# Fewer, longer loads in a two-round decode kernel: 85 transfers where there were 101, and other records kept on the chip

## The chip, the core and the metric

The kernel runs on one core of one Trainium2 chip. The metric is the device time of one execution in microseconds, less is better. The time before is the median of three runs, 712.61 us (712.23 to 714.89). One further execution was recorded by the hardware profiler; all views of the profile in this document are of that execution, or of one like it.

## The reference

One token for each of four batch entries goes twice through the same pair of layers: attention over the last 1,024 positions of a cache, with 32 heads of 128, and a two-matrix MLP with a ReLU. All is float32. What is computed, cut to what matters:

```python
def _A_ref(x, k_cache, v_cache, wq, wo):          # x: 4 x 1 x 640, wq: 640 x 4096, wo: 4096 x 640
    q = (x @ wq).reshape(4, 1, 32, 128).transpose(0, 2, 1, 3)
    k = k_cache[:, :, Sk - W:, :]                 # 4 x 32 x 1024 x 128
    v = v_cache[:, :, Sk - W:, :]
    p = softmax(einsum("bhqd,bhkd->bhqk", q, k) * 128 ** -0.5)
    return einsum("bhqk,bhkd->bhqd", p, v).transpose(0, 2, 1, 3).reshape(4, 1, 4096) @ wo

def _B_ref(x, w1, w2):                            # w1: 640 x 1728, w2: 1728 x 640
    return maximum(x @ w1, 0) @ w2

x = x + _A_ref(layernorm(x), k_cache, v_cache, wq, wo)
x = x + _B_ref(layernorm(x), w1, w2)
x = x + _A_ref(layernorm(x), k_cache, v_cache, wq, wo)
x = x + _B_ref(layernorm(x), w1, w2)
```

## The kernel before

**Records.** The host packs everything that one head needs into a record of `REC` = 9,472 float32 columns on 128 partitions: 640 columns of the query weights, 4,096 of keys (from `K`), 4,096 of values (from `V` = 4,736) and 640 of the output weights (from `WO` = 8,832, "wo" below). One record is 4.85 MB. The two MLP matrices are another 17,280 columns, `wm`. The weights and the cache are needed twice, and the core's memory holds about five and a half records, so nearly all of it is read twice: 32 records and the MLP in round 0, then again in round 1. What is still on the chip when round 1 begins is not read again: round 1 takes the heads in the order 27 to 31, then 0 to 26 (`order`, line 177), so that the last five records of round 0 serve first.

**Places.** `store` (line 139) has five places of one record, `NS`; `home(h, r)` (line 180) gives the place of a record. `ring` (line 142) has 4,832 columns for the MLP's weights of round 0 and for parts of the first new records of round 1. `kept` and `kept2` (lines 140 and 141) hold the last 2,176 columns of records 26 and 5 from round 0 to round 1, entered in `at` (line 186) so that round 1 finds them there.

**Transfers.** All loads are issued on SP's queue, in one fixed order, `items`. The planner code of lines 231 to 283 fills the list before anything is computed: whole records, `group`s that cut several records into longer transfers (`FIVE` cuts five records into three; rows of up to 15,872 columns), the `ending` of a round in smaller pieces, the MLP's pieces (`MLP_RING`, `W1_SLOT`, `W2_SLOT`), and at the start of round 1 a stream that is cut to the places as the five old records leave them (`IN_RING`, `IN_SLOT`, `places`). `pump` (line 285) issues the head of the list as long as its columns are free; `done` and `free` release columns in the program's order as TensorE has read them. SP issues strictly in order: a transfer whose place is not yet free holds all behind it. A consumer waits for the whole transfer that brings its columns.

**Compute.** For each head TensorE makes the query (`query`, PE into `misc`), the scores (`scores`, into one of two `sc_ps`), then after the softmax (`softmax`, `weights`: DVE and ACT) the values (`values`, into `o_ps`), a transposition (`output_T`) and the projection with wo into `acc` (`project`). The loop of line 517 is skewed: in the turn of record n it issues scores of n+1, values of n, query of n+2, `output_T` and `project` of n. In round 0 the wo of the last `LATE` = 6 heads come after everything else of the round, and their projections follow at the end (lines 553 to 560). In the turn of the last but two record four small matmuls of `busy` (line 354) follow the values. `park` (line 326) copies the tail of the last K part out of the spare place into PSUM, so that MLP weights can be loaded there. Then `center` and `mlp` follow; in round 0 the five blocks of w1 free their places one by one, and the next pieces of the MLP are loaded into them.

The same InOrder helper records each instruction, so most rows of the profile have the line L105; groups are told apart by tile names.

Of the kernel before, what the change touches and what calls it, by code (L numbers as in the profile page):

```python
# [32 lines left out]
F32 = mybir.dt.float32  # L33
# [5 lines left out]
P = 128  # L39
B, D, H, DH, W, FF = 4, 640, 32, 128, 1024, 1728  # L40
NB = 4
FD = D // NB
# [5 lines left out]
REC = 2 * D + 8 * W  # L48
# [12 lines left out]
SIXTH = 5  # L61
KEPT2 = WO - 3 * 512
# [24 lines left out]
LAST_FIVE = [REC + 4736, 2 * REC - 4736, REC, REC]  # L87
GROUPS = [{6: FOUR, 10: FIVE, 15: FIVE, 20: FIVE}, {9: FIVE, 14: FIVE, 19: LAST_FIVE}]
# [24 lines left out]
def decode_kernel(ctx: ExitStack, tc: tile.TileContext, xf, rec, wm, out):  # L113
# [65 lines left out]

    def home(h, r):  # L180

        return h % NS if not r or h >= LAST else (h - 6 + LAST) % NS
# [6 lines left out]
    buffers = {"store": store, "ring": ring, "kept": kept, "kept2": kept2}  # L189
# [4 lines left out]
    def place(buf, col):  # L194
        return ("store", spare * REC + FROM + col) if buf == "spare" else (buf, col)
# [11 lines left out]
    def piece(r, h, lo, hi, buf="store", col=None):  # L207
        run(r, h * REC + lo, h * REC + hi, buf, home(h, r) * REC + lo if col is None else col)


    def group(r, h, sizes):
        lo = 0
        for size in sizes:
            run(r, h * REC + lo, h * REC + lo + size, "store", home(h, r) * REC + lo)
            lo += size

    def ending(r, hs, late):
        a, b, c = hs[-3:]
        end = WO if late else REC
        last = WO if late else KEPT  # L220
        for h, lo, hi in ((a, 0, V), (b, 0, V), (a, V, end), (c, 0, V), (b, V, end), (c, V, V + VH), (c, V + VH, last)):
            piece(r, h, lo, hi)
        if late:
            for h in hs[-1:] + hs[-LATE:-1]:
                if h == LAST - 1:
                    piece(r, h, WO, REC, "kept", WO - KEPT)
                else:
                    piece(r, h, WO, REC)
# [3 lines left out]
    piece(0, hs[0], 0, V)  # L232
    piece(0, hs[0], V, REC)
    group(0, 1, FOUR)
    for h in hs[5:-3]:
        if h in GROUPS[0]:
            group(0, h, GROUPS[0][h])
        if any(g <= h < g + sum(z) // REC for g, z in GROUPS[0].items()):
            continue
        piece(0, h, 0, KEPT if h == LAST - 1 else KEPT2 if h == SIXTH else WO if h >= H - LATE else REC)  # L240
        if h == SIXTH:
            piece(0, h, KEPT2, REC, "kept2", 0)
        if h == LAST - 1:
            piece(0, h, KEPT, WO, "kept", 0)
# [10 lines left out]
    for lo, hi, buf, col in IN_RING:  # L255
        piece(1, new[0], lo, hi, *place(buf, col))
    places = [("store", old[i] * REC + lo, old[i] * REC + hi) for i, lo, hi in (
        (0, 0, K), (0, K + 1024, K + VH), (0, K + VH + 1024, V), (1, 0, K + VH), (1, K + VH, V), (0, V, WO), (0, WO, REC),
        (2, 0, V), (1, V, REC), (3, 0, V), (2, V, REC), (4, 0, FROM), (3, V, REC),
        (4, FROM + PARKED, REC), (4, FROM, FROM + PARKED))] + [("ring", 0, RING)]  # L260
    stream = [(new[0], lo, hi) for lo, hi in IN_SLOT] + [(h, 0, KEPT2 if h == SIXTH else REC) for h in new[1:6]]
    for buf, lo, hi in places:
        while stream:
            h, c, end = stream[0]
            cut = max(x for x in [*CUTS, end] if x <= min(end, c + hi - lo))
            if cut <= c:
                break
            piece(1, h, c, cut, buf, lo)
            lo += cut - c
            stream[:1] = [(h, cut, end)] if cut < end else []  # L270
    assert not stream
# [6 lines left out]
    for ks in W1_SLOT:  # L278
        weight(1, ks[0] * FF, (ks[-1] + 1) * FF, "store", home(LAST + 1, 0) * REC + ks[0] * FF)
    n = 0  # L280
    for size in W2_SLOT:
        weight(1, W2 + n * FD, W2 + (n + size) * FD, "store", home(LAST + 2, 0) * REC + n * FD)
        n += size
# [42 lines left out]
    def park(i):  # L326
        a = spare * REC + FROM
        to, lo, hi = ((misc, 0, 512), (sc_ps[1], 512, 1536), (o_ps, 1536, 2048))[i]
        act.copy(to, store[:, a + lo:a + hi])
        free("store", a + lo, a + hi)  # L330
        pump()

    def unpark(i):
        b = home(LAST, 0) * REC
# [6 lines left out]
        if i == 3:  # L341
            c = spare * REC
# [259 lines left out]
```

## Time and profile before

| | before |
|---|---|
| runs, us | 712.23, 712.61, 714.89 |
| profiled execution, us | 711.53 |
| its span, first to last instruction, us | 709.7 |
| PE, DVE, ACT busy, us | 503.7, 317.4, 101.4 |
| read from HBM, MB | 301.61 |
| packets on SP's queue | 14,544 |

The profiled execution took 711.53 us, of which the span is 709.7 us; 1.8 us lie around the span. It is 1.1 us under the median of the runs. Engines in the profile: PE is TensorE's matmul, DVE VectorE, ACT ScalarE, SPq the queue that issues loads. A row of the timeline has the start, the duration, the engine, line, operation, tiles, shape and count, and in brackets the idle time before it and what ended that.

### The profile page before, as it was taken

The page shows a single profiled execution, that of the slowest core. Times are in us where ns is not written, and L with a number is a line of the kernel's source. Part 1 is how long each engine was busy: PE and PEld are TensorE (multiplying, and loading weights), DVE is VectorE, ACT ScalarE, POOL GpSimd, SP SyncE. Part 2 cuts the span into 40 slices and gives each one's busy share as a digit, 9 for nine tenths or more (in the row PEclk, how much of TensorE's full clock was granted, in tenths as well). Part 3 has the DMA queues.
Part 4 walks back from the last instruction along what each step waited for, and adds up shares of the span by engine and source line. Part 5 has one row for each costly group of instructions (what it writes and reads, how often), then busy time and mean ns, then how long its engine had stood idle before and what let it go on. Part 6 is the DMA issues. An engine that isn't in the chain of part 4 may idle for free.

```text
span 709.7 us, 8716 instructions
## 1 busy us (share of the span) xinstructions
PE 503.7 (71%) x3722; PEld 203.4 (29%) x3722; DVE 317.4 (45%) x647; ACT 101.4 (14%) x216; POOL 1.1 (0%) x9
## 2 busy tenths in 40 slices
PE   4388386478566578879878898675577686776885
PEld 2123132232232223333313333231222231233322
DVE  3244253253443453545641866634244252453661
ACT  0111010011010110111120321201011011011120
POOL 0000000000000000000000000000000000000000
PEclk9987787577787776877999999968677676897899
DMA  9999999999999999999999999999999999999997
GB/s 400 421 453 408 454 410 459 417 439 441 428 433 426 424 451 420 424 425 430 427 408 408 417 435 422 448 425 453 428 428 437 439 432 430 432 427 419 427 425 303
DMA packets 14614, 302.24 MB, mean 426 GB/s; under 512 B 1632, under 2 KB 2032, under 8 KB 6256
## 3 DMA queue, kind: packets, MB, share of 16 engines
q1 hardware_dynamic: 14544, 301.69, 99.2%
q8 instruction: 29, 0.48, 0.2%
q14 instruction: 9, 0.07, 0.0%
q10 hardware_dynamic: 32, 0.01, 0.0%
HBM read 301.61 MB, written 0.08 MB: 425 GB/s over the span
## 4 chain that ended last, share of the span: by engine, by line
DMA 73%; PE 21%; DVE 3%; issue 1%; ACT 1%; another core or an unknown queue 0%; SPq 0%; ACTq 0%; DVEq 0%
DMA store<-rec 67%; PE o_ps L105 8%; PE sc_ps L105 7%; DMA store<-wm 3%; DMA ring<-wm 3%; PE misc L105 3%; PE acc L105 3%; DVE scratch L105 1%; DVE o_ps L105 1%; ACT oTs L105 1%; DVE small L105 0%; DVE store L105 0%; PE t_ps L105 0%; SPq L105 0%
## 5 line engine op out<-in xcount | busy, mean ns | idle before, releaser
L105 PE MATMUL sc_ps<-store,qT 128*4 128x512 f32 x1014 | 190.6, 837 | 24.4 <-DMA store<-rec 22.4
L105 PE MATMUL misc<-xT,store 128*128 128x4 f32 x620 | 97.2, 283 | 121.4 <-DMA store<-rec 121.1
L105 PE MATMUL o_ps<-store,scratch 128*16 128x512 f32 x954 | 143.8, 680 | 2.2 <-DMA store<-rec 1.2
L105 PEld LDWEIGHTS misc<-xT,store 128*128 128x128 f32 x620 | 91.8, 230 | 178.5 <-DMA store<-rec 145.7
L105 DVE TENSOR_REDUCE small<-sc_ps 128x1 f32<-128x1024 f32 x64 | 78.3, 1224 | 139.9 <-PE sc_ps L105 139.9
L105 ACT ACTIVATE sc_ps<-sc_ps,small 128x1024 f32<-128x1024 f32 (+1 forms) x68 | 71.1, 1046 | 319.6 <-DVE small L105 318.3
L105 DVE STREAM_TRANSPOSE sc_ps<-sc_ps 128x1024 f32<-128x1024 f32 (+1 forms) x70 | 81.7, 1167 | 0.1
L105 DVE TENSOR_TENSOR qT<-misc,rows 128x4 f32<-128x4 f32 x61 | 9.5, 155 | 135.6 <-PE misc L105 135.6
L105 DVE TENSOR_TENSOR o_ps<-o_ps,of_block 128x512 f32<-128x512 f32 x62 | 43.3, 699 | 52.3 <-PE o_ps L105 50.9
L105 PEld LDWEIGHTS o_ps<-store,scratch 128*16 128x16 f32 x954 | 33.3, 114 | 114.4 <-issue 101.1
L105 PEld LDWEIGHTS sc_ps<-store,qT 128*4 128x4 f32 x1014 | 32.5, 106 | 107.8 <-issue 65.4
L105 PE MATMUL acc<-store,oTs 128*4 128x160 f32 x478 | 34.3, 368 | 17.2 <-ACT oTs L105 16.4
L105 DVE TENSOR_REDUCE scratch<-o_ps 128x128 f32<-128x512 f32 x62 | 42.9, 691 | 2.1
L105 ACT COPY oTs<-o_ps 128x4 f32<-128x4 f32 x62 | 10.1, 162 | 226.6 <-PE o_ps L105 226.6
L105 PE MATMUL o_ps<-rows,scratch 128*128 128x4 f32 x124 | 27.0, 288 | 13.2 <-DVE scratch L105 13.0
L105 PEld LDWEIGHTS o_ps<-rows,scratch 128*128 128x128 f32 x124 | 22.8, 229 | 20.8 <-DVE scratch L105 17.7
L105 DVE TENSOR_TENSOR scratch<-sc_ps,mrt 128x128 f32<-128x128 f32 (+1 forms) x70 | 19.6, 280 | 2.7
L105 DVE TENSOR_SCALAR mrt<-of_batch,small 128x4 f32<-128x4 f32 x64 | 14.7, 229 | 2.2
L105 PE MATMUL acc<-kept,small 128*1 128x344 f32 (+1 forms) x44 | 14.7, 445 | 0.0
L105 PEld LDWEIGHTS acc<-store,oTs 128*4 128x4 f32 x478 | 6.6, 84 | 23.2 <-ACT oTs L105 21.2
L105 DVE STREAM_TRANSPOSE scratch<-small 128x32 f32<-128x32 f32 x64 | 12.8, 201 | 0.8 <-ACT sc_ps L105 0.8
L105 ACT ACTIVATION_READ_ACCUMULATOR sc_ps<-sc_ps,small 128x1 f32 x64 | 12.3, 193 | 0.0
(86 smaller groups left out, 118.1 us busy)
## 6 DMA issues: line engine op xcount, KB each, us to landing
store<-rec SPq DMA_DIRECT2D x10, 7872.0 KB, 28.9
store<-rec SPq DMA_DIRECT2D x5, 7936.0 KB, 33.4
store<-rec SPq DMA_DIRECT2D x14, 2368.0 KB, 27.3
store<-rec SPq DMA_DIRECT2D x6, 4736.0 KB, 26.7
store<-rec SPq DMA_DIRECT2D x4, 6336.0 KB, 27.7
store<-rec SPq DMA_DIRECT2D x2, 7104.0 KB, 29.7
store<-rec SPq DMA_DIRECT2D x2, 6272.0 KB, 43.6
store<-rec SPq DMA_DIRECT2D x2, 4416.0 KB
```

Source lines behind the costliest of these rows:

```text
L105: r = build(*args, **kwargs)
```

## The change

The number of transfers goes from 101 to 85, with the same bytes. Part by part:

- One tile `store` takes the place of `store`, `kept` and `kept2`: `FIRST` = 2,176 columns ahead, five places, 2,176 columns behind. Records 0 to 4 of round 0 lie at column 0 and on, so that the first 2,176 columns of record 0 stay where they were loaded and round 1 finds them there. Records 20 to 24 lie 2,176 columns higher than the others, so that the last 2,176 columns of record 24 end behind the fifth place and stay. Records 26 and 5 are no longer kept. `busy` reads `store`'s first columns in place of `kept`'s.
- Round 0: all records from 0 to 24 come in five groups of `FIVE`, 25 to 27 (27 without wo) in two transfers (`THREE_LATE`), 28 in one, 29 in one, which `ending` before had cut into keys and values with the keys of 30 between them. `LATE` is 5: the wo of record 26 comes with its record and is projected in its turn.
- Round 1: record 0 in four pieces of the ring, two kept parts and its wo; records 1 to 5 as one stream cut to the freed places, across records; 6 to 8 in two transfers (`THREE`) in place of three. Record 24 in one transfer where there were two, record 26 in full. `W1_SLOT` joins blocks 2 and 3.

```diff
-KEPT2 = WO - 3 * 512
+FIRST = K + 3 * 512
...
-IN_RING = [(640, 1152, "ring", 4256), (1152, 3200, "spare", 0), (3200, 4736, "ring", 0), (4736, 6272, "ring", 1536),
-           (6272, 7296, "ring", 3072), (8832, 8992, "ring", 4096)]
-IN_SLOT = [(0, K), (7296, WO), (8992, REC)]
+IN_RING = [(2176, 2688, "ring", 4256), (2688, 4736, "spare", 0), (4736, 6272, "ring", 0), (6272, 8832, "ring", 1536)]
...
-W1_SLOT = [[0, 1], [2], [3], [4]]
+W1_SLOT = [[0, 1], [2, 3], [4]]
...
-LATE = 6
+LATE = 5
...
-FOUR = [REC + 3200, REC + 3072, 2 * REC - 6272]
 FIVE = [REC + 6272, 2 * REC - 3072, 2 * REC - 3200]
 LAST_FIVE = [REC + 4736, 2 * REC - 4736, REC, REC]
-GROUPS = [{6: FOUR, 10: FIVE, 15: FIVE, 20: FIVE}, {9: FIVE, 14: FIVE, 19: LAST_FIVE}]
+THREE = [REC + HALF, REC + HALF]
+THREE_LATE = [REC + 4224, REC - 4224 + WO]
+GROUPS = [{h: FIVE for h in range(0, 25, 5)} | {25: THREE_LATE}, {6: THREE, 9: FIVE, 14: FIVE, 19: LAST_FIVE}]
...
-    store = sb.tile([P, NS * REC], F32, name="store")
-    kept = sb.tile([P, REC - KEPT], F32, name="kept")
-    kept2 = sb.tile([P, REC - KEPT2], F32, name="kept2")
+    store = sb.tile([P, FIRST + NS * REC + REC - KEPT], F32, name="store")
...
     def home(h, r):
-        return h % NS if not r or h >= LAST else (h - 6 + LAST) % NS
+        if r:
+            return FIRST + (h if h >= LAST else h - 6 + LAST) % NS * REC
+        return (0 if h < NS else FIRST + REC - KEPT if h // NS == 4 else FIRST) + h % NS * REC
...
-    at = {("rec", 1, LAST - 1): [(KEPT, REC, "kept", 0)], ("rec", 1, SIXTH): [(KEPT2, REC, "kept2", 0)]}
+    at = {("rec", 1, LAST - 3): [(KEPT, REC, "store", FIRST + NS * REC)], ("rec", 1, 0): [(0, FIRST, "store", 0)]}
...
     def ending(r, hs, late):
         a, b, c = hs[-3:]
         end = WO if late else REC
-        last = WO if late else KEPT
-        for h, lo, hi in ((a, 0, V), (b, 0, V), (a, V, end), (c, 0, V), (b, V, end), (c, V, V + VH), (c, V + VH, last)):
+        for h, lo, hi in ((a, 0, WO if late else KEPT), (b, 0, V), (c, 0, V), (b, V, end), (c, V, V + VH),
+                          (c, V + VH, end)):
             piece(r, h, lo, hi)
...
     hs = order[0]
-    piece(0, hs[0], 0, V)
-    piece(0, hs[0], V, REC)
-    group(0, 1, FOUR)
-    for h in hs[5:-3]:
+    for h in hs[:-3]:
         if h in GROUPS[0]:
             group(0, h, GROUPS[0][h])
...
+    piece(0, hs[-4], 0, WO)
     ending(0, hs, True)
...
-    stream = [(new[0], lo, hi) for lo, hi in IN_SLOT] + [(h, 0, KEPT2 if h == SIXTH else REC) for h in new[1:6]]
+    cuts = [h * REC + x for h in new[1:6] for x in CUTS]
+    c, end = new[1] * REC, new[6] * REC
     for buf, lo, hi in places:
...
+        if lo == old[0] + WO:
+            piece(1, new[0], WO, REC, buf, lo)
+        elif c < end:
+            cut = max(x for x in cuts if x <= min(end, c + hi - lo))
+            run(1, c, cut, buf, lo)
+            c = cut
...
-            pe.matmul(to[32 * g:32 * g + 1, :n], ones, kept[:, :n], start=to is not spare_cols, stop=True,
+            pe.matmul(to[32 * g:32 * g + 1, :n], ones, store[:, :n], start=to is not spare_cols, stop=True,
```

More of the change, by code (lines that the diff above doesn't have):

```diff
@@ L194, in place @@
     def place(buf, col):
-        return ("store", spare * REC + FROM + col) if buf == "spare" else (buf, col)
+        return ("store", spare + FROM + col) if buf == "spare" else (buf, col)
     def weight(r, lo, hi, buf, col):
@@ L224, in ending @@
             for h in hs[-1:] + hs[-LATE:-1]:
[L225 to L228, printed above, removed]
+                piece(r, h, WO, REC)
     hs = order[0]
-    piece(0, hs[0], 0, V)
-    piece(0, hs[0], V, REC)
-    group(0, 1, FOUR)
-    for h in hs[5:-3]:
+    for h in hs[:-3]:
         if h in GROUPS[0]:
             group(0, h, GROUPS[0][h])
[L238 to L244, printed above, removed]
+    piece(0, hs[-4], 0, WO)
     ending(0, hs, True)
@@ L256, in decode_kernel @@
         piece(1, new[0], lo, hi, *place(buf, col))
[L257 to L260, printed above, removed]
-    stream = [(new[0], lo, hi) for lo, hi in IN_SLOT] + [(h, 0, KEPT2 if h == SIXTH else REC) for h in new[1:6]]
-    for buf, lo, hi in places:
[L263 to L271, printed above, removed]
+    places = [("store", old[i] + lo, old[j] + hi) for i, lo, j, hi in (
+        (0, 0, 0, K), (0, K + 1024, 0, K + VH), (0, K + VH + 1024, 0, V), (1, 0, 1, K + VH), (1, K + VH, 1, V),
+        (0, V, 0, WO), (0, WO, 0, REC), (2, 0, 2, V), (1, V, 1, REC), (3, 0, 3, V), (2, V, 2, REC), (3, V, 4, FROM),
+        (4, FROM + PARKED, 4, REC), (4, FROM, 4, FROM + PARKED))] + [("ring", 0, RING)]
+    cuts = [h * REC + x for h in new[1:6] for x in CUTS]
+    c, end = new[1] * REC, new[6] * REC
+    for buf, lo, hi in places:
+        if lo == old[0] + WO:
[4 more added lines that the diff above has]
+            c = cut
+    assert c == end
     for h in new[6:-3]:
@@ L326, in park @@
     def park(i):
-        a = spare * REC + FROM
+        a = spare + FROM
         to, lo, hi = ((misc, 0, 512), (sc_ps[1], 512, 1536), (o_ps, 1536, 2048))[i]
@@ L341, in unpark @@
         if i == 3:
-            c = spare * REC
+            c = spare
             at["rec", 1, H - 1] = [(0, FROM, "store", c), (FROM, V, "store", a), (V, V + 1024, "store", b + K),
```

13 lines of the change are left out of this document (6 added, 7 removed).

## The prediction

> **What bounds the kernel now.** I read the page first: slices, queues, the chain of waits.
>
> ```profile
> span 709.7 us, 8716 instructions
> ...
> DMA  9999999999999999999999999999999999999997
> ...
> q1 hardware_dynamic: 14544, 301.69, 99.2%
> ...
> DMA 73%; PE 21%; DVE 3%; issue 1%; ACT 1%; another core or an unknown queue 0%; SPq 0%; ACTq 0%; DVEq 0%
> ```
>
> SP's queue keeps the DMA engines busy for 99.2% of the span, and no slice but the last falls under nine tenths. No compute engine is near that: 27% of the chain is not DMA only because a transfer is issued when TensorE has freed its place. Next, the same by stages (columns: window, PE, PEld, DVE, ACT, POOL busy, granted clock, DMA share, GB/s):
>
> ```profile
> 100.00:350.00 250.00, 179.69 (x1207) 72.30 (x1205) 110.58 (x210) 32.67 (x71) 0.00 (x0) 0.77 1.00 431
> ...
> 390.00:400.00 10.00, 8.39 (x68) 3.59 (x67) 9.11 (x26) 5.43 (x10) 0.00 (x0) 1.00 1.03 408
> ...
> 460.00:680.00 220.00, 155.07 (x1066) 62.53 (x1070) 94.83 (x185) 27.36 (x60) 0.00 (x0) 0.77 1.00 431
> ...
> 702.00:704.00 2.00, 0.10 (x6) 0.04 (x8) 0.00 (x0) 0.00 (x0) 0.00 (x0) 1.00 0.79 328
> 704.00:706.00 2.00, 2.00 (x58) 1.56 (x60) 0.00 (x0) 0.00 (x0) 0.00 (x0) 1.00 0.41 162
> ```
>
> The stream has no hole until 702; then the last loads land and TensorE follows them. So the time is: start, the stream's own busy time, about 5 us of tail. The change can move it in two ways only: by what the stream costs beside its bytes, and by holes.
>
> **The change, part by part.**
>
> *Bytes: nothing.* Two times 2,176 columns stay on the chip before and after. Counted from the planner's lists, both come to 589,216 columns, 301.7 MB, as the queue's row says.
>
> *Sixteen transfers fewer.* Each has 128 rows and, by 14,544 / 101, 144 packets in all. What one packet costs beside its bytes I take from windows with long and with short transfers:
>
> ```profile
> q1 hardware_dynamic: 1589, 77.71, 99.8%
> ...
> q1 hardware_dynamic: 1956, 25.56, 99.8%
> ...
> q1 hardware_dynamic: 4888, 24.73, 101.1%
> ```
>
> These are SP's queue in 460 to 640, 640 to 700 and 350 to 410 us: packets, MB, share. Busy time is 179.64, 59.88 and 60.66 us. With a us per MB and c us per packet, the first two give 59.88 - (25.56 / 77.71) x 179.64 = 0.79 us for 1956 - 523 = 1,433 packets, so c = 0.55 ns and 0.080 us a transfer. The first and third give 3.49 us for 4,382 packets, 0.80 ns, 0.115 us a transfer; in that window fetches of instructions and late issues add to it, so I take the lower: 16 x 0.080 = **1.3 us less**, up to 1.8. By place: four fewer in records 0 to 9 of round 0, four to the end of its records, six at the entry of round 1, two at its end.
>
> *Joined groups in the steady part.* Here a transfer must be issued before the one ahead has landed; call the difference its lead. What lead is needed: the store of the output, 80 KB, takes 1.6 us from issue to landing, of which 0.2 us is data at 431 GB/s, so 1.4 us.
>
> ```profile
> out<-scratch SPq DMA_DIRECT2D x1, 80.0 KB, 1.6
> ...
> 572.96 0.33 SPq L105 DMA_DIRECT2D store<-rec  x1
> ...
> 548.72 30.73 DMA store<-rec
> ```
>
> The second row is a tight issue of before: the transfer ahead, issued at 548.72, landed 30.73 later, at 579.45; lead 6.5 us. The groups from record 10 to 19 of round 0 and from 9 to 23 of round 1 keep their cuts and the readers that free them, so these leads stay. New ones:
>
> ```profile
> 60.61 2.30 PE L105 MATMUL misc<-xT,store 128*128 128x4 f32 x10 [2.46 <-DMA store<-rec]
> ...
> 238.15 1.90 PE L105 MATMUL o_ps<-store,scratch 128*16 128x512 f32 x16
> 247.12 2.30 PE L105 MATMUL misc<-xT,store 128*128 128x4 f32 x10 [7.07 <-DMA store<-rec]
> ...
> 463.10 2.30 PE L105 MATMUL misc<-xT,store 128*128 128x4 f32 x10 [5.99 <-DMA store<-rec]
> ...
> 466.62 3.53 PE L105 MATMUL sc_ps<-store,qT 128*4 128x512 f32 x16
> 469.98 1.45 PE L105 MATMUL o_ps<-ring,scratch 128*16 128x512 f32 x9
> ```
>
> Record 21's group now waits for the first half of record 18's values (2,176 columns more): about 239.2 by the second row, against a landing at 247.1, lead 7. In round 1 the group of record 9 must wait for half of record 5's values, which come after the query and scores of record 6. Those now arrive with the first half of record 7, 5.6 us later than at 463.1: 468; as in the last three rows the half is through 7.7 us after the query began, 475.7. The transfer ahead (7.5 records) lands 16.8 us after 468, at 484.8: lead 9, where it was issued at once before. All leave the stream whole; a cost of 0, and bounds of 0 on both sides as long as a lead stays over 1.4.
>
> *The start.* The first transfer is 15,744 columns, not 4,736, so record 0 comes 13 us later; the third transfer still ends after 47,360 columns, the landing at 60.6.
>
> ```profile
> 1.74 0.98 ACTq L105 DMA_DIRECT2D scratch<-xf  x3
> ...
> q10 hardware_dynamic: 32, 0.01, 0.7%
> ...
> 9.64 0.87 PE L102 MATMUL acc<-scratch,ring 128*128 128x160 f32 x2 [9.64 <-DMA scratch<-xf]
> ...
> 16.67 1.89 PE L105 MATMUL sc_ps<-store,qT 128*4 128x512 f32 x8
> ...
> 29.43 2.29 PE L105 MATMUL misc<-xT,store 128*128 128x4 f32 x10 [10.87 <-DMA store<-rec]
> ...
> 40.49 3.25 PE L105 MATMUL sc_ps<-store,qT 128*4 128x512 f32 x10
> ```
>
> TensorE's first work waits for x until 9.64 although its loads were issued by 2.7; their 32 packets (second row, ACT's queue in 4 to 10 us) take turns with SP's rows. If the turns are counted in rows, some 9 rows of 15,744 columns (2.33 us each at 431 / 16 GB/s) pass first: 24 us, 14.4 later than before. The scores of record 0, before done at 18.6, are done at 33.0; record 1, before held to 29.43, is already there. The stretch from 29.43 to 40.49 (11.1 us: query 1 to projection 0) then ends at 44.1, and scores of 2 and values of 1 at 3 us each at 50.5. That frees the fourth transfer: lead 60.6 - 50.5 = 10. Cost 0, and 0 at both ends up to a delay of 8.7 us.
>
> *The end of round 0.* Here I see a cost. Record 29 comes whole, ahead of the keys of 30.
>
> ```profile
> 305.34 1.66 PE L105 MATMUL misc<-xT,store 128*128 128x4 f32 x10 [1.32 <-DMA store<-rec]
> ...
> 311.63 2.52 PE L105 MATMUL o_ps<-store,scratch 128*16 128x512 f32 x16
> ...
> 327.99 1.28 PE L105 MATMUL misc<-xT,store 128*128 128x4 f32 x10 [0.58 <-DMA store<-rec]
> ...
> 332.49 2.35 PE L105 MATMUL o_ps<-store,scratch 128*16 128x512 f32 x16
> 334.77 1.28 PE L105 MATMUL misc<-xT,store 128*128 128x4 f32 x10
> ...
> 340.52 1.28 PE L105 MATMUL misc<-xT,store 128*128 128x4 f32 x10
> ...
> 346.10 2.48 PE L105 MATMUL acc<-kept,small 128*1 128x344 f32 x8
> 349.70 0.50 PE L105 MATMUL misc<-xT,store 128*128 128x4 f32 x3 [1.12 <-DMA store<-rec]
> ```
>
> Record 28 lands at 327.95 (third row), afterwards at 328.2 (640 columns of wo 26 more, 0.76 us, less about seven transfers saved). Record 29, whole, is 8,832 columns or 10.5 us behind: 338.7. Before, its keys came first and its query ran at 334.77. The projection of record 26, now in its turn, costs TensorE 0.5 us ahead of 330, where it then waits for loads. From 338.7 TensorE needs one record without a projection (305.34 to 314.15, less 0.8 for it: 8.0 us), the next (6.9 us as from 327.99, 5.8 as from 340.52) and the four busy matmuls (2.3 us): the query of record 31 begins at about 355.3, not at 349.70. Call it S.
>
> ```profile
> 359.53 1.05 PE L105 MATMUL sc_ps<-store,scratch 128*16 128x512 f32 x8 [1.03 <-DMA store<-rec]
> ...
> 366.40 0.91 PE L105 MATMUL sc_ps<-ring,xT 128*4 128x432 f32 x8 [0.94 <-DMA ring<-wm]
> ...
> 367.36 3.85 SPq L105 DMA_DIRECT2D ring<-wm  x3
> ...
> 371.99 0.53 PE L105 MATMUL sc_ps<-store,xT 128*4 128x432 f32 x1 [1.16 <-DMA store<-wm]
> ```
>
> Without its waits (1.0 us at 359.53, 0.9 for wo, 0.9 for w1) the path from that query to the first freed block of w1 is 367.36 - 349.70 - 2.8 = 14.9, say 15.1 us: issue at S + 15.1 = 370.4. The load ahead landed at 371.95 and will land 0.65 earlier (eight transfers fewer up to there), at 371.3; less 1.4 the issue must come by 369.9. That leaves a hole of **0.5 us**. Ends: 0, if TensorE runs that record at its short times (S = 352.5); 2.1, if both records and the busy matmuls take the long ones (S = 357). I take 0.5, since every wait of over 1.3 us in these rows was followed by the long times.
>
> On this the Trainium skill has a rule, "TensorE: Matmul & The Clock Gate", Part 1: the array falls to half clock after an idle window of about 3.4 us and needs a busy one to recover. TensorE will idle 2 to 4 us ahead of record 29, so by that rule it depends on how the windows fall whether S is 352.5 or 355.3: 1.3 us gained or 0.8. The rows side with the slow case: 1.32 us of idle at 305.34 was enough.
>
> *The MLP of round 0, entry and end of round 1.* Same pieces, same readers; loads and TensorE follow each other there, both 0.65 us earlier plus the hole. At the entry the pieces of records 1 and 2 are cut otherwise; the tightest loses 0.4 us of lead against the same reader. With a share of 1.03 in 390 to 400 I set 0, at most 0.4. At the end blocks 2 and 3 of w1 land together, 0.9 us late for block 2, but behind them TensorE waits for w2 in any case. The tail keeps its 5 us.
>
> *Sum:* -1.3 + 0.5 = **-0.8 us**: 711.53 becomes 710.7. The median of the runs lies 1.1 above the profiled execution, so 712.61 - 0.8 = **711.8** for the runs. One half per cent, 3.6 us, is about what a measurement of this kernel can tell from no change; the forecast lies within it.
>
> **The rivals.**
>
> *A. No hole.* S near 352.5: 712.6 - 1.3 (to 1.8), 711.3 to 710.8. For it: leads in the MLP were under 5 us before and no hole came of it. Against it: the long times after a wait.
>
> *B. The end of round 0 runs wholly at the long times.* Both records, the four busy matmuls and the path to w1's first block late: S = 361.4 (two records of 9 us and 4.7 us), hole 361.4 + 15.1 - 369.9 = 6.6; 712.6 - 1.3 + 6.6 = 717.9, **slower**. It is slower than before from S = 356.1 on, by over half a per cent from 359.7. For it: long times lasted until 334 after the wait at 317. Against it: they never outlasted two records.
>
> *C. The start.* If x or record 0 came only with the second transfer (41 us), the fourth would be issued near 66, 7 us after it is needed: 712.6 - 1.3 + 7 = 718.3. Against it: x waited for no more than some nine rows.
>
> *D. The saved packets do not set the time,* because engines of the sixteen that end earlier carry them: 0 + 0.5, 713.1. Against it: a mean share of 1.00 over whole stages leaves no engine time to spare.
>
> *E. Each transfer holds the stream for its issue and landing.* At 1.4 us each (the output's store), 16 fewer would give 22 us: 690.2. Against it stand the rows of the price: 0.08 us of stream for one. The Trainium skill, "DMA: Bandwidth & Descriptors", Anatomy of one DMA, fits a fixed 2.0 us a DMA, by which the same mechanism would give 32 us (an estimate); it calls most of that completion latency, which a full queue hides, and the trace agrees.
>
> **Chances.** Forecast 0.50, A 0.20, D 0.12, B 0.10, C 0.03, E 0.01; 0.04 for what I don't see. Faster by over 0.5% (under 709.0) can come from E and stray runs alone: 0.03. Slower by over 0.5% (above 716.2): B, C and part of the unseen, 0.13. Within: 0.84. The range goes from A with the dearer packets (712.6 - 1.8, less 0.5 of scatter: 710.3) to D with the longest hole of the bounds and as much scatter (712.6 + 2.1 + 0.3: 715.0).
>
> **What will show it.** The queue's packets should be 12,240 with the same MB, its busy time 1.3 us less. The query ahead of 30's scores should start near 346, that of 31 near 355, and the fifth load of the MLP be issued near 370. A DMA share well under 1.00 anywhere between 20 and 700 us would make the forecast wrong, above all in 366 to 372 or in 50 to 80; a span shorter by over 2 us would say that a transfer costs more than its packets.

## The result, and the profile after

| | before | after |
|---|---|---|
| median, us | 712.61 (711.98 to 714.89, 9 runs) | 716.31 (714.15 to 717.68, 9 runs) |
| ratio to before, 95% interval | | 1.0040 [1.0028, 1.0052] |
| profiled execution, us | 711.53 | 714.98 |
| its span, us | 709.7 | 713.3 |

The change makes the kernel slower, by 0.2 to 0.4%. Timed twice more in later stretches, the same kernel had a median of 714.08 against 712.78, ratio 1.0019 [1.0005, 1.0034], and of 715.35 against 712.74, ratio 1.0027 [1.0010, 1.0044]. The forecast was 711.8 with a range up to 715.0; the 716.31 lies outside it, as does the 715.35, and the 714.08 inside. A stretch is a time in which kernels are timed together. Its ratios and the differences of its medians part by up to 1.3 us (e14 below), so both are given where it matters.

The page after, with the lines that answer to those shown of before:

```profile
span 713.3 us, 8680 instructions
...
GB/s 396 438 415 449 431 422 441 441 423 431 447 417 434 447 420 430 437 420 428 424 390 394 394 433 424 448 443 437 426 429 442 426 437 430 433 428 428 423 423 267
...
q1 hardware_dynamic: 12240, 301.68, 98.7%
```

The packets fell as foreseen, from 14,544 to 12,240, but the queue's busy time did not: 98.7% of 713.3 us is 704.0 us, and before 99.2% of 709.7 was 704.0 us too. The row of GB/s points at the place: three slices around 357 to 410 us carry 390 to 394 GB/s.

The same by stages. The columns are window, busy PE, PEld, DVE, ACT and POOL, granted clock, DMA share, GB/s. First before, where its rows were not shown yet, then after:

```profile
0.00:99.00 99.00, 58.06 (x359) 24.92 (x363) 37.52 (x85) 12.76 (x25) 1.13 (x9) 0.84 0.99 424
0.00:100.00 100.00, 59.06 (x364) 25.09 (x364) 38.18 (x86) 12.76 (x25) 1.13 (x9) 0.85 1.00 427
...
364.00:380.00 16.00, 11.08 (x107) 3.32 (x107) 2.47 (x10) 2.27 (x5) 0.00 (x0) 1.00 1.01 408
390.00:412.00 22.00, 19.86 (x178) 8.46 (x177) 17.97 (x41) 8.16 (x16) 0.00 (x0) 1.00 1.03 424
```

```profile
0.00:99.00 99.00, 51.12 (x342) 22.37 (x342) 36.17 (x80) 12.58 (x24) 1.12 (x9) 0.88 1.00 427
0.00:100.00 100.00, 52.12 (x346) 23.37 (x346) 36.45 (x82) 12.58 (x24) 1.12 (x9) 0.87 0.99 425
100.00:350.00 250.00, 173.79 (x1205) 67.15 (x1205) 109.76 (x211) 31.59 (x70) 0.00 (x0) 0.79 1.00 432
364.00:380.00 16.00, 11.86 (x128) 4.14 (x125) 4.21 (x14) 3.68 (x9) 0.00 (x0) 1.00 0.97 381
390.00:412.00 22.00, 20.41 (x176) 7.77 (x172) 16.48 (x37) 7.06 (x14) 0.00 (x0) 0.92 1.00 399
```

Bytes not moved in a window, at the rate of before, are time that the end has to make up: 16 x 27 / 408 = **1.1 us** lost in the MLP of round 0 and 22 x 25 / 424 = **1.3 us** at the entry of round 1; 460 to 680 runs at 431 GB/s in both. The windows of the first 350 us tell of no loss and no gain of that size: their ends cut through rows of 63 KB, which take 2.3 us each, and the first window that has 427 against 425 GB/s when it ends at 100 us has 424 against 427 when it ends at 99. The two losses make 2.4 us, and the last load comes 1.8 us later, which the rows of the tail show (the last group of matmuls on w2, before and then after; the bracket has the idle time ahead and what ended it):

```profile
703.96 2.79 PE L105 MATMUL acc<-store,scratch 128*4 128x160 f32 x68 [1.90 <-DMA store<-wm]
```

```profile
705.78 4.54 PE L103 MATMUL acc<-store,scratch 128*4 128x160 f32 x68 [1.09 <-DMA store<-wm]
```

They begin at 703.96 and 705.78, 1.8 us apart, and last 2.79 and 4.54 us, another 1.75. Together they are the 3.6 us between the spans. The 1.75 goes with the clock of this one execution: the granted clock was 0.52 there (the last column but two), and before 0.98 in 704 to 709. In two more profiles of the changed kernel (e12 and e13 below) the group took 2.79 and 2.78 us.

```profile
703.00:710.00 7.00, 5.91 (x90) 3.07 (x84) 0.00 (x0) 0.00 (x0) 0.00 (x0) 0.52 0.48 198
```

What happened ahead of the MLP of round 0 is on TensorE's timeline after (the queries of records 29, 30 and 31, the values of 29, the busy matmuls, the first work on w1, and the waits for it), then on SP's (issue times of the load that is awaited at 372 and of the one behind it, the refill), and last, before, the first of these issues and two of the same waits:

```profile
339.41 1.28 PE L103 MATMUL misc<-xT,store 128*128 128x4 f32 x10 [3.47 <-DMA store<-rec]
...
344.18 2.07 PE L103 MATMUL o_ps<-store,scratch 128*16 128x512 f32 x16
346.18 1.28 PE L103 MATMUL misc<-xT,store 128*128 128x4 f32 x10
...
351.82 2.48 PE L103 MATMUL acc<-store,small 128*1 128x344 f32 x8
354.23 1.28 PE L103 MATMUL misc<-xT,store 128*128 128x4 f32 x10
...
368.20 0.91 PE L103 MATMUL sc_ps<-ring,xT 128*4 128x432 f32 x8 [0.27 <-DVE xT L103]
...
372.09 0.53 PE L103 MATMUL sc_ps<-store,xT 128*4 128x432 f32 x1 [0.55 <-DMA store<-wm]
...
374.19 0.53 PE L103 MATMUL sc_ps<-ring,xT 128*4 128x432 f32 x1 [0.63 <-DMA ring<-wm]
...
377.08 0.53 PE L103 MATMUL sc_ps<-ring,xT 128*4 128x432 f32 x1 [1.42 <-DMA ring<-wm]
```

```profile
365.63 0.33 SPq L103 DMA_DIRECT2D store<-wm  x1
369.17 2.77 SPq L103 DMA_DIRECT2D ring<-wm  x3
```

```profile
361.74 0.33 SPq L105 DMA_DIRECT2D store<-wm  x1
...
374.09 0.53 PE L105 MATMUL sc_ps<-ring,xT 128*4 128x432 f32 x1 [0.63 <-DMA ring<-wm]
...
376.14 0.53 PE L105 MATMUL sc_ps<-ring,xT 128*4 128x432 f32 x1 [0.58 <-DMA ring<-wm]
```

TensorE waits 3.47 us for record 29 and does not catch up. Before, the first work on w1 at 366.40 had waited for its load; now at 368.20 it waits for DVE, the load being there. So the place of that block is freed and refilled at 369.17 and not at 367.36. The transfer ahead of the refill lands just before 372.09: a **lead** (landing of the transfer ahead less issue) of 2.9 us, where it was 371.99 - 367.36 = 4.6 us before. The refill itself lands almost in time (374.19 against 374.09 before), but the one behind it 0.9 us late (377.08 against 376.14). From here on TensorE and the loads wait for each other in turns. The load ahead of the refill is late too: it was issued at 365.63 and not at 361.74, yet landed in time.

### The profile page after: what moved, and what is told of

It reads as the page before. It is cut to its first block, busy times and chain, and to the rows that moved or that the text cites. A ratio compares the mean times of both kernels' runs of the same rounds, so it can differ in the third digit from the quotient of the medians.

```text
span 713.3 us, 8680 instructions
## 1 busy us (share of the span) xinstructions
PE 494.7 (69%) x3722; PEld 199.4 (28%) x3722; DVE 317.5 (45%) x647; ACT 101.3 (14%) x216; POOL 1.1 (0%) x9
## 3 DMA queue, kind: packets, MB, share of 16 engines
q1 hardware_dynamic: 12240, 301.68, 98.7%
## 5 line engine op out<-in xcount | busy, mean ns | idle before, releaser
L103 PE MATMUL sc_ps<-store,qT 128*4 128x512 f32 x1022 | 186.1, 816 | 48.4 <-DMA store<-rec 46.0
L103 PE MATMUL misc<-xT,store 128*128 128x4 f32 x620 | 93.9, 278 | 99.6 <-DMA store<-rec 99.4
L103 PE MATMUL o_ps<-store,scratch 128*16 128x512 f32 x962 | 145.8, 673 | 2.1 <-DVE scratch L103 1.9
L103 PEld LDWEIGHTS misc<-xT,store 128*128 128x128 f32 x620 | 88.5, 223 | 157.4 <-DMA store<-rec 121.3
L100 PE MATMUL acc<-scratch,ring 128*128 128x160 f32 x2 | 0.9, 540 | 22.4 <-DMA scratch<-xf 22.4
L103 PE MATMUL acc<-store,small 128*1 128x344 f32 (+1 forms) x44 | 14.7, 445 | 0.0
```

What stands on the lines that cost most here:

```text
L100: r = build(*args, **kwargs)
L103: r = build(*args, **kwargs)
```

## The experiments

Lead is taken in the same way everywhere: start of the first work on the block that waits at 372, less the issue at 367 to 371. "Before" is in each case the kernel before, run in the same stretch (26 to 35 runs). A lead is read from one profiled execution, a time from 6 to 12 executions.

### The end of round 0: undone, and made alone

*e1 and e14: the changed kernel, with its end of round 0 loaded as before* (one transfer more than the change):

```diff
-        for h, lo, hi in ((a, 0, WO if late else KEPT), (b, 0, V), (c, 0, V), (b, V, end), (c, V, V + VH),
-                          (c, V + VH, end)):
+        first = ((a, 0, V), (b, 0, V), (a, V, end)) if late else ((a, 0, KEPT), (b, 0, V))
+        for h, lo, hi in first + ((c, 0, V), (b, V, end), (c, V, V + VH), (c, V + VH, end)):
```

> The changed kernel with the end of round 0 loaded as before: keys of record 29, keys of 30, then values of 29 (86 transfers). Theory 1, the end of round 0 makes TensorE late for the first block of w1: the query of record 31 goes back from 354.2 to about 350, the fifth load of the MLP is issued near 366.8, the extra delay of landings that grows from 0.7 to 1.5 us between 364 and 378 is gone, and the time falls by 1.5 to 3 us, to 713.3 to 714.8. Rival, the loss lies in the entry of round 1 and the tail: under 0.7 us less.

> The changed kernel with the end of round 0 loaded as before. Theory 1: 712.5 to 713.3, and 1.0 to 2.5 us below the changed kernel of the same stretch. Rival (the end of round 0 is worth 0.5): within 0.7 us of it.

*e13: the changed kernel, in the stretch of e14.* Its text:

> The changed kernel, unaltered, timed in one stretch with the same kernel whose end of round 0 is loaded as before (next row). Theory 1 (a lead of 2.9 us at the first freed block of w1 leaves holes of 1.5 to 2.5 us; lead = landing of the transfer ahead less issue): 1.0 to 2.5 us above that kernel, 714.0 to 715.5 here. Rival (the first measurement of the changed kernel was high by chance, the end of round 0 costs the 0.5 us of the prediction): 712.9 to 713.6, within 0.7 us of it.

e1 took 713.28 us, ratio 1.0005 [0.9991, 1.0019]; e14 713.09, 0.9987 [0.9973, 1.0002]; e13, beside e14, 715.35. So this one cut is worth 715.35 - 713.09 = **2.3 us** by the medians of one stretch, 2.9 by the ratios. The rival, 0.7 us or less, falls. In e14's profile (SP's issue, TensorE's first work on the waiting block):

```profile
367.41 3.87 SPq L103 DMA_DIRECT2D ring<-wm  x3
```

```profile
372.06 0.53 PE L103 MATMUL sc_ps<-store,xT 128*4 128x432 f32 x1 [1.16 <-DMA store<-wm]
```

The lead is back at 4.65 us, and the window of the MLP at 403 GB/s.

e13 shows the other direction. The rows are the query of 29, the values behind it, the query of 31, TensorE's first work on the waiting block and its last wait for w1; then SP's two issues, then the window:

```profile
339.44 1.49 PE L103 MATMUL misc<-xT,store 128*128 128x4 f32 x10 [4.37 <-DMA store<-rec]
...
344.66 3.15 PE L103 MATMUL o_ps<-store,scratch 128*16 128x512 f32 x16
...
355.79 1.28 PE L103 MATMUL misc<-xT,store 128*128 128x4 f32 x10
...
372.11 0.53 PE L103 MATMUL sc_ps<-store,xT 128*4 128x432 f32 x1
...
378.62 0.53 PE L103 MATMUL sc_ps<-ring,xT 128*4 128x432 f32 x1 [2.01 <-DMA ring<-wm]
```

```profile
367.19 0.33 SPq L103 DMA_DIRECT2D store<-wm  x1
370.73 2.77 SPq L103 DMA_DIRECT2D ring<-wm  x3
```

```profile
364.00:380.00 16.00, 12.14 (x116) 3.82 (x108) 4.76 (x16) 3.93 (x8) 0.00 (x0) 1.00 0.89 330
```

In this execution TensorE waited longer for record 29, and its values behind the wait ran longer (3.15 us, against 2.07 in the first profile). The granted clock shows it, first in the first profile after, then in e13: TensorE ran at half clock for longer.

```profile
344.60:347.10 2.50, 2.50 (x25) 1.16 (x17) 1.80 (x2) 1.20 (x2) 0.00 (x0) 1.00 1.00 426
```

```profile
344.60:347.10 2.50, 2.50 (x16) 0.51 (x12) 1.23 (x1) 0.89 (x1) 0.00 (x0) 0.50 0.98 419
```

The refill was issued 1.6 us later still. Its lead is at most 372.11 - 370.73 = 1.4 us, the very value that the prediction held sufficient, and the window carries 330 GB/s, a DMA share of 0.89. Not all of that is the refill's: the load ahead of it was issued at 367.19, 5.5 us later than before, and by the packets of the trace the 16 DMA engines stand idle for 0.9 us on average ahead of 368.5 too, where before they don't. How late TensorE is changes from run to run, which goes with the changed kernel's wide spread in this stretch (712.23 to 717.52, e14: 711.36 to 714.20).

*e4: the kernel before, with only the end of round 0 changed* (record 29 whole, ahead of the keys of 30; 100 transfers):

```diff
-        for h, lo, hi in ((a, 0, V), (b, 0, V), (a, V, end), (c, 0, V), (b, V, end), (c, V, V + VH), (c, V + VH, last)):
+        first = ((a, 0, WO), (b, 0, V)) if late else ((a, 0, V), (b, 0, V), (a, V, end))
+        for h, lo, hi in first + ((c, 0, V), (b, V, end), (c, V, V + VH), (c, V + VH, last)):
```

> The kernel before with one part of the change alone: record 29 whole ahead of the keys of 30 (100 transfers). Theory 1: the query of record 31 starts near 354, the time rises by 1.5 to 3 us, to 714.1 to 715.6. Rival: within 0.7 us of before.

Measured 714.20, ratio 1.0024 [1.0015, 1.0034]: this cut alone makes the kernel before 1.5 us slower by the medians, 1.7 by the ratio. Issue and first work on the block:

```profile
368.86 2.77 SPq L105 DMA_DIRECT2D ring<-wm  x3
```

```profile
372.14 0.53 PE L105 MATMUL sc_ps<-store,xT 128*4 128x432 f32 x1 [0.90 <-DMA store<-wm]
```

### Is it TensorE's lateness, or the cut itself?

*e9: the changed kernel, without the four busy calls of round 0*, so with the same loads and an earlier TensorE; *e12: the changed kernel, in the same stretch:*

```diff
-            if end:
+            if end and r:
                 for _ in range(4):
                     busy()
```

> The changed kernel without the four busy matmul calls of record 29's turn in round 0, which there stand in no wait any more. Theory 1, it is TensorE's lateness at the first block of w1 that costs: the query of record 31 starts near 351.8 and not 354.2, the first freed block is issued near 367, the lead goes from 2.9 back over 4.5 us, and 1 to 2 us of the loss come back against the changed kernel in the same call. Rival, the order of the loads itself costs (values of 29 ahead of the keys of 30): under 0.5 us come back.

> The changed kernel once more, for the comparison in this call: 2.0 to 3.7 us over before, as measured.

e9 took 713.16 us, ratio 1.0003 [0.9992, 1.0014]; e12 714.08, 1.0019 [1.0005, 1.0034]. Taking away 2.5 us of TensorE's work (the row at 351.82 above), with each load as it was, gives 0.9 us back by the medians. e12 itself is 1.3 us over before, less than the 2.0 to 3.7 expected. The 0.9 lies between the 1 to 2 us of theory 1 and the 0.5 of its rival, and the two intervals overlap, so this pair alone does not decide. Its refill was issued in time:

```profile
367.33 3.02 SPq L103 DMA_DIRECT2D ring<-wm  x2
```

*e10, e15 and e16: the kernel before, all loads unchanged, with four, five and two busy calls ahead of the MLP of round 0:*

```diff
     def mlp(r):
...
+        if not r:
+            for _ in range(4):
+                busy()
```

> The kernel before, loads untouched, with four busy matmul calls ahead of the MLP of round 0, which hold TensorE for 2.5 us: the first block of w1 is freed near 369.1 and not 367.4, as in the changed kernel. Theory 1: the lead falls to about 2.9 us and the time rises by 1 to 2 us, although 2.9 is twice the 1.4 us that the prediction held to be enough. Rival, a lead over 1.4 us is enough: within 0.4 us of before.

> The kernel before with five busy calls ahead of the MLP of round 0, so that the first freed block of w1 is issued some 1.7 us later, lead about 2.9, as in the changed kernel, and every transfer is as before. Theory 1: 1.5 to 2.5 us slower than before, 714.2 to 715.2, and a share of DMA at 0.96 to 1.00 in 360 to 372. Rival (only a lead under 1.4 us costs anything): 712.5 to 713.2.

> The kernel before with two busy calls at that place: they fit almost into TensorE's wait of 0.9 us, so the issue is late by 0 to 0.4 us, lead 4.2 to 4.6. Theory 1: 0 to 0.5 us slower, 712.7 to 713.3. If busy calls cost time by themselves and not by lateness (a second rival): 0.5 to 0.9, by two fifths of what five cost.

Issue and first work on the block, in e10, e15 and e16 in turn:

```profile
368.68 2.75 SPq L105 DMA_DIRECT2D ring<-wm  x3
```

```profile
372.06 0.53 PE L105 MATMUL sc_ps<-store,xT 128*4 128x432 f32 x1 [1.02 <-DMA store<-wm]
```

```profile
369.15 2.75 SPq L105 DMA_DIRECT2D ring<-wm  x3
```

```profile
371.89 0.53 PE L105 MATMUL sc_ps<-store,xT 128*4 128x432 f32 x1 [0.38 <-DMA store<-wm]
```

```profile
367.59 3.69 SPq L105 DMA_DIRECT2D ring<-wm  x3
```

```profile
372.06 0.53 PE L105 MATMUL sc_ps<-store,xT 128*4 128x432 f32 x1 [1.16 <-DMA store<-wm]
```

Now all of them side by side, and with them the other runs but e8 and e11, which cut other transfers; GB/s are those of the window 364 to 380, and the last two columns compare with the kernel before of the same stretch:

| kernel | lead, us | GB/s | median less before's, us | ratio, 95% interval |
|---|---|---|---|---|
| before | 4.6 | 408 | | |
| e6, before with a filled tail | 4.6 | 406 | -0.12 | 0.9998 [0.9989, 1.0007] |
| e3, change with old end and start | 4.7 | 400 | 0.43 | 1.0012 [1.0002, 1.0023] |
| e1, change with the old end | 4.7 | 402 | 0.63 | 1.0005 [0.9991, 1.0019] |
| e14, the same again | 4.65 | 403 | 0.35 | 0.9987 [0.9973, 1.0002] |
| e9, change without the busy calls | 4.6 at most | 399 | 0.38 | 1.0003 [0.9992, 1.0014] |
| e16, before with 2 busy calls | 4.5 | 402 | 0.01 | 0.9992 [0.9980, 1.0004] |
| e5, e3 with another entry | 4.1 | 401 | 0.31 | 1.0002 [0.9988, 1.0016] |
| e10, before with 4 | 3.4 | 390 | 1.75 | 1.0018 [1.0005, 1.0031] |
| e4, before with the new end | 3.3 | 382 | 1.55 | 1.0024 [1.0015, 1.0034] |
| e2, change with the old start | 3.0 | 383 | 1.54 | 1.0026 [1.0011, 1.0041] |
| e12, change, second time | 3.0 | 384 | 1.30 | 1.0019 [1.0005, 1.0034] |
| after, first profile | 2.9 | 381 | 3.70 | 1.0040 [1.0028, 1.0052] |
| e15, before with 5 | 2.7 | 391 | 2.02 | 1.0018 [1.0006, 1.0030] |
| e7, change with a filled tail | 1.6 at most | 350 | 1.60 | 1.0031 [1.0019, 1.0043] |
| e13, change, third time | 1.4 at most | 330 | 2.61 | 1.0027 [1.0010, 1.0044] |

e16 shows that busy calls cost nothing as long as they fill waits; e10 and e15 that 1.3 and 1.8 us of lateness (368.68 and 369.15 against 367.36), without any other change, make the kernel slower. In these two the load ahead of the refill was issued as early as before (362.47 and 361.63), so the refill alone is late. The lead that this place needs lies between 3.4 and 4.1 us.

The trace also shows what the late refill does. In 368.6 to 369.6 us the DMA share is 0.97 before and 0.66 in e15 (0.60 in e10); in 369.5 to 370.1 it is 1.08 before and 0.55 after:

```profile
368.60:369.60 1.00, 1.00 (x10) 0.17 (x2) 0.00 (x0) 0.00 (x0) 0.00 (x0) 1.00 0.97 356
369.50:370.10 0.60, 0.51 (x5) 0.10 (x6) 0.00 (x0) 0.00 (x0) 0.00 (x0) 1.00 1.08 426
```

```profile
368.60:369.60 1.00, 1.00 (x8) 0.41 (x10) 0.16 (x1) 0.00 (x0) 0.00 (x0) 1.00 0.66 273
```

```profile
369.50:370.10 0.60, 0.60 (x11) 0.11 (x6) 0.28 (x2) 0.25 (x1) 0.00 (x0) 1.00 0.55 230
```

So DMA engines run dry 2 to 3 us ahead of the landing near 371.6. By the packets of the trace eight of the 16 stand idle at 370.0 us, after as in e15, while the others still move the transfer ahead; before, 15 or 16 are busy. The refill's first packet starts 0.96 us after its issue (after, e10 and e15 alike). The two together ask for a lead of 3 to 4 us (2 to 3 and 0.96; an estimate), which fits the table. Averaged over the 16 engines, the idle time from 368.5 to 371 is 0.3 to 0.7 us in e2, e4, e10, e12, e15 and after, and under 0.1 in each row of the table with a lead over 4 us.

That is less than these kernels lose. In e15 a later window, 390 to 400 us, shows a larger loss, but it can't be put down to the lead: e8 below, with a lead of up to 4.7 us, has the same granted clock of 0.68 there and loses much of the same (e15 first, then e8). Where the rest of the loss comes from stays open.

```profile
390.00:400.00 10.00, 9.12 (x54) 3.08 (x57) 6.20 (x20) 4.33 (x8) 0.00 (x0) 0.68 0.85 305
```

```profile
390.00:400.00 10.00, 9.12 (x54) 2.87 (x50) 6.80 (x19) 4.33 (x8) 0.00 (x0) 0.68 0.92 340
```

### The start

*e2: the changed kernel, with records 0 to 4 of round 0 in five transfers as before; e3: e1 and e2 together.*

```diff
-GROUPS = [{h: FIVE for h in range(0, 25, 5)} | {25: THREE_LATE}, {6: THREE, 9: FIVE, 14: FIVE, 19: LAST_FIVE}]
+GROUPS = [{h: FIVE for h in range(5, 25, 5)} | {0: [V, V, REC + 3200, REC + 3072, 2 * REC - 6272]} | {25: THREE_LATE},
+          {6: THREE, 9: FIVE, 14: FIVE, 19: LAST_FIVE}]
```

> The changed kernel with records 0 to 4 loaded as before, in five transfers and not three (87 transfers). Theory 2, the first rows of 63 KB cost the slowest DMA engine half a microsecond: landings at 190 to 230 us come 0.3 to 0.5 us earlier and the time falls by 0.5. Rival, that is scatter: 0.15 us more for two transfers.

> Both undone, 88 transfers. If the two account for the loss and the sixteen saved transfers are worth 1.3 us as priced, 13 of them give 1.0 us: 711.6, against 712.6 before. If the entry of round 1 or the tail carries a loss of its own, 713 or more.

e2 took 714.19, ratio 1.0026 [1.0011, 1.0041]; e3 713.08, 1.0012 [1.0002, 1.0023]. Against e1 in the same stretch, e3 is 0.2 us lower by the median and higher by the ratio: no effect of the start on the time can be told. The traces tell a little: the landing that a query awaits near 247 us comes at 247.10 to 247.51 in seven profiles with the new start (after, e1, e7, e9, e12, e13, e14), mean 247.35; at 246.88 to 247.21 in e2, e3 and e5, mean 247.07; and at 246.91 to 247.31 in six with the start of before (before, e4, e6, e10, e15, e16), mean 247.05. So the new start makes this landing 0.3 us later, the least of what theory 2 had.

### The price of a transfer

*e8 and e11: the kernel before, with each group of five records cut into 10 and into 20 transfers where there were 3* (136 and 186 transfers; same places, same readers):

```diff
-FIVE = [REC + 6272, 2 * REC - 3072, 2 * REC - 3200]
+FIVE = 10 * [HALF]
```

```diff
-FIVE = [REC + 6272, 2 * REC - 3072, 2 * REC - 3200]
+FIVE = 5 * [2176, 2560, 2048, 2688]
```

> The kernel before with each five-record group of the steady parts in ten transfers and not three: 136 transfers, the same bytes. By the price of 0.080 us for one, 35 more cost 2.8 us (4.0 at 0.115): 715.4 to 716.7. Rival, saved or added packets do not set the time: under 0.5 us more.

> The kernel before with each five-record group in twenty transfers and not three: 186 transfers, the same bytes. At 0.080 us a transfer 85 more cost 6.8 us; at what the run with 136 transfers showed, 1.3 us for 35 or 0.037, 3.1 us.

Measured 714.24, ratio 1.0017 [1.0007, 1.0026], and 716.74, ratio 1.0051 [1.0032, 1.0069]: e8 lies between what its text had for the price and for the rival, e11 near the price that e8 gave. By the ratios 35 transfers cost 1.2 us and 85 cost 3.6: **0.035 and 0.043 us each** (0.037 and 0.047 by the medians). Even the upper ends of the intervals, 0.053 and 0.058, lie under the 0.080 of the prediction. SP's queue on the two pages:

```profile
q1 hardware_dynamic: 19584, 301.69, 99.1%
```

```profile
q1 hardware_dynamic: 26784, 301.69, 99.4%
```

The packets' busy time rises as the prediction priced it: 99.1% of 713.5 us and 99.4% of 715.4 us are 707.1 and 711.1, less 704.0 makes 0.088 and 0.084 us a transfer. Only half of that reaches the end. These runs add transfers to the steady part; that a transfer saved elsewhere is worth as much is assumed.

### The entry of round 1

*e5: e3, with 512 columns fewer put into the third freed place of the entry's stream*, so that this transfer lands earlier and the one behind it has 0.6 us less lead:

```diff
-        (0, 0, 0, K), (0, K + 1024, 0, K + VH), (0, K + VH + 1024, 0, V), (1, 0, 1, K + VH), (1, K + VH, 1, V),
+        (0, 0, 0, K), (0, K + 1024, 0, K + VH), (0, K + VH + 1024, 0, V - 512), (1, 0, 1, K + VH), (1, K + VH, 1, V),
```

> The kernel of e3_both (88 transfers) with 512 columns less in the third place that round 1 fills at its entry; the stream makes them up later, with as many transfers. Theory 3, in the entry SP's lead over the landing ahead (2.5 to 5 us) is too short, and each column less of it becomes a hole: the lead at the next transfer falls by 0.6 us, idle and slowed time in 390 to 412 us rises from 0.9 to about 1.5 us, time 0.4 to 0.6 up from 713.1. Rival, a lead over 1.4 us costs nothing: within 0.2 us.

Measured 713.24, ratio 1.0002 [0.9988, 1.0016], against e3's 1.0012 [1.0002, 1.0023] in another stretch; the theory that too small a lead in this place makes the entry slow is not borne out.

How much the new entry costs at all is not shown. In 390 to 412 us the profiles of before, e4, e6, e10 and e16, which have the old entry, show 410 to 424 GB/s, mean 415; the ten of the changed kernel and of e1, e2, e3, e5, e7, e9 and e14 show 395 to 422, mean 406. That would be 22 x 9 / 415 = 0.5 us. But e8 and e11 have the old entry too, with 389 and 400 GB/s, and with them the mean falls to 409 and the difference to 0.2 us. The times say as little: e1, e3, e5, e9 and e14 have the new entry and a full lead at w1, and their ratios average 1.0002, where 13 to 16 saved transfers at 0.04 us would give 0.9993. Either the entry costs these 0.6 us (e3's text would read its 713.08 so) or the saved transfers do not bring them.

### The tail

*e6 and e7: the kernel before and the changed kernel, with five busy calls in the waits for w2 in round 1's MLP*, to keep the last projections from the long times of the profile after:

```diff
             for i, size in enumerate(sizes):
+                if r:
+                    for _ in range((3, 2, 0, 0)[i]):
+                        busy()
```

> The kernel before with five more busy matmul calls in the MLP of round 1, where TensorE waits for w2. Theory 4, in a part of the runs the clock drops to half in that wait and the last projections take 4.5 and not 2.8 us: the median falls by 0.3 to 1 us from 712.65 and the slowest runs come down by 1.7. Rival, the tail's clock is no part of the scatter: same median, or up to 1 us more where the added matmuls run at half clock.

> The changed kernel with the same five calls. Its profiled execution had the half clock at the end. Theory 4: the median falls by 0.5 to 1.7 us from 716.3. Rival: no fall.

Measured 712.81, ratio 0.9998 [0.9989, 1.0007], and 714.53, ratio 1.0031 [1.0019, 1.0043]. The first gains nothing; the second rests on six runs and lies between the measurements of the changed kernel. No share of the tail in the result is shown. No version here beats the kernel before: the lowest ratio, 0.9987 [0.9973, 1.0002] of e14, does not exclude 1, and the same kernel was at 1.0005 as e1.

## Why the prediction was wrong

*The hole at w1 is the step that failed, by its size.* The prediction put the query of record 30 near 346, that of 31 at 355.3, and the refill of the first freed block at 370.4: they came at 346.18, 354.23 and 369.17. The lateness was foreseen, with its cause. Wrong was the sentence that a transfer needs a lead of 1.4 us, taken from the output's store, the one small transfer that runs when nothing else moves. By it the refill at 369.17 was in time and should have cost nothing. In the stream a lead of 3.4 us already costs 1.75 us (e10; 1.3 by the ratio), and the new end as a whole costs 1.5 to 2.3 (e4; e13 against e14) where 0.5 was priced and 2.1 was the upper bound. That lateness alone is enough is shown by e10 and e15 beside e16. What the 1.4 us left out is on the traces: engines that finished their share of the transfer ahead run dry 2 to 3 us before its landing. The prediction looked at the refill only; that the load ahead of it would be issued late as well (365.63 and in e13 367.19, against 361.74) it did not have. Of the 1.5 to 2.3 us about 1 shows in the window of the MLP; where the rest arises is open.

*Saved packets, -1.3 us.* Too large by half or more: at 0.035 to 0.043 us, 16 transfers are worth 0.6 to 0.7 us (e8, e11), if saving is worth what adding costs. The busy time of an added transfer was right; that a saturated queue passes all of it on to the end was not, and in the changed kernel itself the queue's busy time did not fall (704.0 us in both profiles). Rival D, to which the prediction gave 0.12, holds at least half of the truth. Record 29, set at 338.7 with seven saved transfers, was there at 339.41, and the load that was to land 0.65 us earlier, at 371.3, at 372.09, 0.1 us later than before.

*Joined groups of the steady part, 0.* Right as far as the windows can tell: 432 and 431 GB/s after, 431 twice before.

*The start, 0.* The mechanism came as described: x, whose packets take turns with rows three times as long, was there at 22.4 us (24 predicted, 9.64 before), and no stall of the kind of rival C came of it. (A slip in the working, 44.1 and two times 3 being 50.1 and not 50.5, changes nothing there.)

```profile
L100 PE MATMUL acc<-scratch,ring 128*128 128x160 f32 x2 | 0.9, 540 | 22.4 <-DMA scratch<-xf 22.4
```

The landing near 247 us came 0.3 us later on average, which the prediction had not, and e2, e3 and e5 undo it; no effect on the time is told from it.

*The entry of round 1, 0 with at most 0.4.* Neither borne out nor refuted: something between 0 and 0.6 us. e5 changed the lead in one place only, and the cuts of the whole stream were not tried one by one.

*The tail keeps its 5 us.* Right; the 1.75 us of the first profile after went with a granted clock of 0.52, which e12 and e13 do not have in the last matmuls.

*The rivals.* A (no hole) falls. B was the right side by another road: TensorE did not run late for two records at the long times (S, the query of 31, was 354.2 to 355.8, not 361.4), but less lateness than B needed was enough. C falls, D holds by half or more. E falls clearly: 85 transfers more cost 3.6 us, not 119. On that the Trainium skill, "DMA: Bandwidth & Descriptors", Anatomy of one DMA, says that its fixed 2.0 us, fitted on GpSimd's path and not on SP's queue, are mostly completion latency. That a full queue hides such a latency is not on that page; here the 0.035 to 0.043 us show it.

*The sum, mended.* The kernels with the new entry, 13 to 16 transfers fewer and a full lead stand at 1.0002 of before on average, +0.1 us; the end of round 0 adds 1.5 to 2.3. That makes +1.6 to +2.4 us. The three measurements were +3.7, +1.3 and +2.6 us by the medians, +2.9, +1.4 and +1.9 by the ratios; the height of the first one is not explained.

The prediction weighed the Trainium skill, "TensorE: Matmul & The Clock Gate", Part 1 (half clock after an idle window of about 3.4 us) for S. The trace agrees: after a wait of 3.47 us the granted clock was back at 1.00 by 344.6, after one of 4.37 us it was still 0.50 until 347.1, the values took 2.07 and 3.15 us, and S differs by 1.6 us. Whether the longer wait or the place of the windows made the difference, these two executions do not tell.

## What to carry to other kernels

The lead that a transfer needs in a saturated stream is not the latency of one transfer, since the engines that share the transfer ahead finish at different times: look for the smallest lead in the kernel before that demonstrably leaves no hole, here 4.6 us (4.1 in e5), and treat whatever falls below it as priced by experiment. Where each load waits for a place that compute frees, and compute waits for loads in turn, 1.3 to 1.8 us of work ahead of that loop cost 1.3 to 2.0 us here, so the pieces just ahead of it should stay small and their order kept. A transfer more in such a stream cost some 0.04 us, and one stage made late costs as much as some forty to sixty of them. And where rows are long, a window's GB/s hang on its ends: move an end by 1 us before you believe a difference.

## What was not expected of the hardware

- A transfer more adds 0.084 to 0.088 us of packets' busy time on the queue, yet only 0.035 to 0.043 us to the time (35 and 85 transfers more).
- DMA engines run dry while the transfer ahead is still landing: with the refill issued at 369.15 and not at 367.36, the share in 368.6 to 369.6 us falls from 0.97 to 0.66 (e15), though the load ahead lands near 371.6 in both.
- A window of 16 us falls from 403 to 330 GB/s when two loads of w1 are issued late (362.59 against 367.19, and 367.41 against 370.73; e14 and e13), though the first of them still lands in time.
- After a wait of 3 to 4 us for a load, the same 16 matmuls of 512 columns took 2.07 us in one execution and 3.15 in another, with a granted clock of 1.00 and 0.50 in 344.6 to 347.1. The two reach the query of record 31 1.6 us apart (354.23 and 355.79).
